# Two PSUM banks taken as one tile for a linear-attention head pair, and the split work and loads reordered around it

## The chip, the cores and the metric

The kernel runs on one core of a Trainium2 chip. The metric is the device time of one execution, in microseconds. Engines are called PE (TensorE, matrix products), DVE (VectorE), ACT (ScalarE), POOL (GpSimd) and SP (SyncE, which here only issues DMAs). PSUM is the memory that PE's products go to; a one-bank tile here has 512 fp32 values per partition.

## The reference, cut to what matters

```python
# q, k, v: (8 batches, 8 heads, 576 positions, 64)
kv = np.einsum('bhsd,bhse->bhde', k, v)
out = np.einsum('bhsd,bhde->bhse', q, kv)
rms = np.sqrt(np.mean(out * out, axis=-1, keepdims=True) + 1e-06)
x = (out / rms * g_norm)            # then (B,H,S,D) -> (B*S, H*D) = 4608 x 512
h = x @ w_in                        # w_in 512 x 2048
sp = np.maximum(h, 0.0) + np.log1p(np.exp(-np.abs(h)))
g = h * erf(sp)
return g @ w_out                    # w_out 2048 x 512
```

Attention without softmax: per head a 64x64 product of k and v, q times it, a normalisation over the 64 channels. Then a two-layer network with the activation h * erf(softplus(h)).

## The kernel before, in words

**Tokens.** They are worked in nine groups T of 512 columns. T=0 to 7 are the first 512 positions of each batch; T=8 holds the remaining 64 positions of all eight batches, whose attention outputs are collected in `x_last`. Everything is kept transposed: channels on partitions, tokens along the free axis.

**Precision.** T=0 runs its network in plain fp32. From T=1 on, f>=2 (`WHOLE`), each fp32 operand is written as fp32r forms (an upper part, a lower part, a combination), and `product` (L443 to 463) makes a 128x512 block as 12 fp32r matmuls: eight into `n_ps`, four into `m_ps`. DVE adds the two (`add` L439, `add_scaled` L434). The forms of an operand are made by ACT (upper, L399) and DVE (lower and combination, L402, L405). The weights' forms are made in the T=1 stage, by `w_upper` on ACT (L423) and `w_lower` on DVE (L426, L429), and written to DRAM; from then on `load_parts` (L589) fetches them block by block on SP's queue.

**Stages.** The main loop (L638 to 735) takes n = 0 to 31: T=0 for n<16, T=1 for n=16 to 31, with f = n mod 16 the block of 128 hidden channels. Then come the periods m = 8 to 36, four per group for T=2 to 8 (L780 to 853). A period has four hidden blocks (x times w_in; the softplus and erf on ACT; h times the result on DVE, L848) and four result blocks of the period before it (h times w_out).

**Attention.** While group T is worked, the attention of T+1 is made, one pair of heads p at a time (four pairs per group): a pair per period, and in the T=1 stage a pair at f = 0, 4, 8 and 12. Its pieces are those that `attention` (L265 to 394) returns:
- `products`: k times v into `kv_ps` (L293), for even pairs also a transpose of the q of the last 64 positions (L301); DVE copies the two 64x64 blocks into the block-diagonal `bd_kv` (L308) and, in even pairs, the transposed tail q (L311); PE transposes the q of 512 positions into `qt_ps` (L315) and ACT copies it out (L316).
- `apply`: `bd_kv` times the tail (L320, 64 columns) and times qT (L321, 512 columns, into `se_ps`), in fp32; DVE copies the tail's result to `x_last` (L322), ACT squares the rest (L324).
- `halve`: DVE splits the squares into two fp32r parts (L334, L335). `mean`: PE averages over channels (L342, L343, into `ms_ps`); ACT takes logarithm, exponential and square (L354 to 356). `norm`: three DVE instructions end in x (L362, L365, L374). `split`: the forms of x (L399, L402, L405).

`kv_ps`, `qt_ps`, `se_ps` and `ms_ps` are one-bank tiles that take turns in a pool of two. The remaining six banks serve the blocks.

**Order.** Nothing is reordered by a scheduler: each engine runs its instructions in the order in which the code calls them (`manual_schedule`). Semaphore waits are added where one engine touches a tile that another has written or read. In a period the pieces stand at places:

```python
places = (0, 2, 3, 5, 6, 8)      # products, apply, halve, mean, norm, split; place i+1 is behind block i
FETCH = ("", "in", "in", "out", "in", "out", "in", "out out")
```

So products come ahead of the first hidden block, apply behind the second, halve behind the third, mean behind the first result block. The split of a period's x comes behind its last result block, that is, in the queues of ACT and DVE just ahead of what the next products ask of them. The k, v and q of two pairs on are issued on SP's queue by `products_and_loads` (L387), at place 0.

In the T=1 stage each step f calls: the pieces due, the hidden block, ACT's copy of h and softplus (L702), the gating of an earlier block, `w_lower` of the blocks begun and `w_upper` of the blocks in `to_cut[f]`, then pieces again. `places_w` (L616) names the steps in which w_out blocks are split that stay in a place of their own in SBUF.

Of the kernel before, what the change touches and what calls it, by code (L numbers as in the profile page):

```python
# [39 lines left out]
FP32 = mybir.dt.float32  # L40
# [3 lines left out]
AF = mybir.ActivationFunctionType  # L44
ALU = mybir.AluOpType
PSUM = bass.MemoryType.PSUM
# [14 lines left out]
def kernel(  # L61
# [31 lines left out]
    first_w = room.enter_context(tc.tile_pool(name="first_w", bufs=1, side="right"))  # L93
    gate = room.enter_context(tc.tile_pool(name="gate", bufs=7, side="right"))
    early = early_room.enter_context(tc.tile_pool(name="early", bufs=2))
    ps_at = ctx.enter_context(tc.tile_pool(name="ps_at", bufs=2, space=PSUM))
    ps_h = ctx.enter_context(tc.tile_pool(name="ps_h", bufs=2, space=PSUM))
    ps_o = ctx.enter_context(tc.tile_pool(name="ps_o", bufs=1, space=PSUM))

    ctx.enter_context(tc.manual_schedule())  # L100

# [160 lines left out]

    xT, x_forms, tails = {}, {}, {}

    def attention(T, p, pools=None):  # L265

        st = {}

        halves = FIRST <= T < B
        bd = bd_kv[:, (T * NP + p) % 2, :]  # L270

        q_tail, o_tail = slice(P, 2 * P), slice(2 * P, 2 * P + R)

        def bank(name):
            pool, tag = (pools or {}).get(name, (ps_at, "at"))
            return pool.tile([P, G], FP32, name=name, tag=tag)

        def square_tile(name):

            if T == 0:  # L280
                return gate.tile([P, G], FP32, name=name, tag="h")
            return attp.tile([P, G], FP32, name=name, tag="qT")

        def products():

            kv_ps = st["kv"] = bank("kv_ps")
            ks, vs, qs = (x.pop((T, p)) for x in (k_sb, v_sb, q_sb))
            C = chunks(T)
            for c in range(C):
                rows = slice(0, S // C + (c < S % C))  # L290
                for i in range(2):
                    s = slice(i * D, i * D + D)
                    nc.tensor.matmul(  # L293
                        kv_ps[s, s],
                        lhsT=ks[rows, i, c],
                        rhs=vs[rows, i, c],
                        start=(c == 0),
                        stop=(c == C - 1),
                    )
            if p % 2 == 0:  # L300
                nc.tensor.transpose(kv_ps[:, q_tail], q_last[:, p // 2], ident)  # L301
            if p == NP - 2:
                for i in range(NP):
                    load_last(T + 1, i)
            st["qT"] = square_tile("qT")
            for i in range(2):
                s = slice(i * D, i * D + D)
                nc.vector.tensor_copy(out=bd[s, s], in_=kv_ps[s, s])  # L308
            if p % 2 == 0:
                tails[T] = attp.tile([P, P], FP32, name="qT_last", tag="t")  # L310
                nc.vector.tensor_copy(out=tails[T], in_=kv_ps[:, q_tail])  # L311
            st["tail"] = tails[T][:, p % 2 * R : p % 2 * R + R]
            qt_ps = bank("qt_ps")
            for j in range(J):
                nc.tensor.transpose(qt_ps[:, j * P : j * P + P], qs[:, j], ident)  # L315
            nc.scalar.copy(st["qT"], qt_ps)  # L316

        def apply():
            qT, o_ps, kv_ps = st["qT"], bank("se_ps"), st.pop("kv")
            nc.tensor.matmul(kv_ps[:, o_tail], lhsT=bd, rhs=st.pop("tail"), start=True, stop=True)  # L320
            nc.tensor.matmul(o_ps, lhsT=bd, rhs=qT, start=True, stop=True)  # L321
            nc.vector.tensor_copy(out=x_last[:, p, T * R : T * R + R], in_=kv_ps[:, o_tail])  # L322
            st["o"] = o_ps
            nc.scalar.activation(qT, o_ps, AF.Square)  # L324

        def square():
            st["o"], st["qT"] = x_last[:, p, :], square_tile("sq")
            nc.scalar.activation(st["qT"], st["o"], AF.Square)

        def halve():  # L330
            sq = st.pop("qT")
            hi = st["hi"] = attp.tile([P, G], FP32R, name="sq_hi", tag="rms_r")
            lo = st["lo"] = attp.tile([P, G], FP32R, name="sq_lo", tag="sq_lo")
            nc.vector.tensor_copy(out=hi, in_=sq)  # L334
            nc.vector.tensor_tensor(out=lo, in0=sq, in1=hi.bitcast(FP32), op=ALU.subtract)  # L335

        def mean(table=True):
            ms = st["ms"] = bank("ms_ps")
            if halves:


                nc.tensor.matmul(ms, lhsT=mean_w, rhs=st.pop("hi"), start=True, stop=False)  # L342
                nc.tensor.matmul(ms, lhsT=mean_w, rhs=st.pop("lo"), start=False, stop=True)  # L343
                u = square_tile("u")
            else:
                u = st.pop("qT")
                nc.tensor.matmul(ms, lhsT=mean_w.bitcast(FP32), rhs=u, start=True, stop=True)
            if T > 0:
                r = attp.tile([P, G], FP32, name="rms_r", tag="rms_r")
                exp_ln_table()  # L350
            else:
                r = gate.tile([P, G], FP32, name="rms_r", tag="s")
            st["u"], st["r"] = u, r
            nc.scalar.activation(r, ms, AF.Ln, bias=eps_col)  # L354
            nc.scalar.activation(r, r, AF.Exp, scale=-0.5)
            nc.scalar.activation(u, r, AF.Square)
            if table and (T > 0 or p == NP - 1):
                softplus_table()

        def norm():  # L360
            ms, u, r = (st.pop(name) for name in ("ms", "u", "r"))
            nc.vector.scalar_tensor_tensor(  # L362
                out=u, in0=ms, scalar=EPS, in1=u, op0=ALU.add, op1=ALU.mult
            )
            nc.vector.scalar_tensor_tensor(  # L365
                out=u, in0=u, scalar=3.0, in1=r, op0=ALU.subtract, op1=ALU.mult
            )
            if T < FIRST:
                if T not in xT:
                    xT[T] = wide.tile([P, KC, G], FP32, name="xT", tag="h")  # L370
                x = xT[T][:, p, :]
            else:
                x = st["x"] = x_new.tile([P, G], FP32, name="x", tag="x")
            nc.vector.scalar_tensor_tensor(  # L374
                out=x,
                in0=st.pop("o"),
                scalar=gm_col,
                in1=u,
                op0=ALU.mult,
                op1=ALU.mult,  # L380
            )

        def split():
            if T >= FIRST:
                thirds(st.pop("x"), *(form[:, p] for form in x_forms[T]))

        def products_and_loads():  # L387
            products()
            load_pair(T * NP + p + 2)

        if T == 0:
            return products, apply, halve, mean, norm
        first = (products_and_loads, apply) if T < B else (lambda: None, square)
        return (*first, halve if halves else lambda: None, mean, norm, split)


    def upper(x, high):
# [215 lines left out]

    others = [("in", f) for f in range(WHOLE)]
    others += [("out", f) for f in (*range(FC - BATCH, FC), *range(FC - BATCH))]
    places_w = {4: 0, 5: 1, 8: 0, 9: 1, FC - 4: 0, FC - 3: 1}  # L616
    to_cut = {f: [] for f in range(FC)}
    for f in range(FC):
        if f < FC - BATCH:
            to_cut[f] = [("in", f + WHOLE), others.pop(0)]  # L620
        elif f == FC - BATCH:
            to_cut[f] = [("in", FC - 2), ("in", FC - 1)]
        if f in places_w:
            to_cut[f].append((*others.pop(0), places_w[f]))
# [13 lines left out]
    for n in range(FIRST * FC + 1):  # L638
        T, f = divmod(n, FC)
        if n == FC:  # L640
            early_room.close()
            late = ctx.enter_context(tc.tile_pool(name="late", bufs=1))
            x_new = ctx.enter_context(tc.tile_pool(name="x_new", bufs=1))
            acc = ctx.enter_context(tc.tile_pool(name="acc", bufs=1))
            w_in_p = ctx.enter_context(tc.tile_pool(name="w_in_p", bufs=BATCH))
            low = low_room.enter_context(tc.tile_pool(name="low", bufs=1))
            forms = late.tile([P, 3, KC, G], FP32R, name="x_forms0")
            x_forms[FIRST] = [forms[:, i] for i in range(3)]
# [43 lines left out]
        if T < FIRST:  # L692
# [6 lines left out]
            else:  # L699
                nc.scalar.activation(h, n_ps, AF.Copy, scale=SHIFT - 1.0)  # L700
                add(h, m_ps)
            nc.scalar.activation(s, h, AF.Softplus)  # L702
            if T == FIRST - 1:
                if f == 1:
                    x_both = wide.tile([P, KC, G], FP32R, name="x_both", tag="h")
# [5 lines left out]
                    w_lower(*key)  # L711
                for key in to_cut[f]:
                    w_upper(*key)
            if n == 0:
                w_next("split")
            for piece in steps[f][1]:
# [63 lines left out]
    for m in range(first_batch, batches + 1):  # L780
# [9 lines left out]
        def piece():  # L790
            if todo:
                todo.pop(0)()
# [95 lines left out]
```

## Time and profile before

| | |
|---|---|
| median of 11 runs | 959.39 us (957.81 to 960.97) |
| profiled execution | 961.9 us, span 960.1 us |
| mean granted PE clock | 0.996 |
| busy: PE, DVE, ACT | 932.9, 740.8, 616.1 us |
| DMA | 259.78 MB, mean 271 GB/s |
| start of a period's k-v product to the next | 24.84 and 24.72 us in turn (m=10 on) |
| attention of the T=1 stage starts at | 146.69, 175.23, 206.06, 236.38 us |
| m=8 and m=9 start at | 261.89 and 286.74 us |

Times in the profile are microseconds from the start of the span. A timeline row is: start, duration, engine, line, operation, output tile <- input tiles, shapes, count, and in brackets how long the engine stood idle before it and what ended that. A row of waits is: engine, tile and line that waited, what it waited for, total us, times, longest. PEld is PE's loading of weights, SPq the issue of a DMA on SP's queue.

### The profile page before, as it was taken

What the parts mean: (1) busy time and instruction counts of PE and PEld (TensorE: products, weight loads), DVE (VectorE), ACT (ScalarE), POOL (GpSimd) and SP (SyncE); (2) the same over time, 40 slices, a digit from 0 to 9 for tenths busy, and PEclk for the clock granted to TensorE, in tenths of its full rate; (3) what the DMA queues carried; (4) which work ended last, traced back from release to release, by engine and by line L of the source; (5) the groups of instructions that cost most, each with busy time, mean ns of one, the idle gap of its engine ahead of it and who ended that gap; (6) DMA issues with size and microseconds to landing.
All of it is one profiled execution on the core that took longest, in us unless ns stands there. A gap on an engine that the chain in (4) does not pass through costs nothing.

```text
span 960.1 us, 11752 instructions
## 1 busy us (share of the span) xinstructions
PE 932.9 (97%) x4272; PEld 686.4 (71%) x4272; DVE 740.8 (77%) x1054; ACT 616.1 (64%) x825; POOL 2.4 (0%) x10
## 2 busy tenths in 40 slices
PE   6999999989998999999999999999999999999998
PEld 4344445556586888888888888888888788878886
DVE  2979958777675888888878887878787877778667
ACT  3889875677663666666666666666666666665552
POOL 0000000000000000000000000000000000000000
PEclk9999999999998999999999999999999999999999
DMA  9756505688899887889888978988897779768872
GB/s 253 262 159 216 174 10 233 228 317 303 293 306 329 312 310 276 249 306 339 296 261 322 325 289 279 322 316 289 271 341 266 262 244 352 274 258 298 338 273 67
DMA packets 111842, 259.78 MB, mean 271 GB/s; under 512 B 43864, under 2 KB 69544, under 8 KB 111784
## 3 DMA queue, kind: packets, MB, share of 16 engines
q1 hardware_dynamic: 110152, 256.73, 76.1%
q10 hardware_dynamic: 1568, 2.29, 0.8%
q8 instruction: 34, 0.56, 0.2%
q14 instruction: 24, 0.20, 0.1%
q0 software_dynamic: 64, 0.00, 0.0%
HBM read 224.40 MB, written 34.60 MB: 270 GB/s over the span
## 4 chain that ended last, share of the span: by engine, by line
PE 79%; DVE 8%; ACT 8%; DMA 3%; issue 1%; SPq 0%; DVEq 0%; ACTq 0%
PE n_ps L456 42%; PE m_ps L456 21%; PE o_ps L514 5%; PE h_ps L685 3%; PE se_ps L321 2%; PE kv_ps L293 2%; PE qt_ps L315 1%; DMA out_dram<-e 1%; DMA w_out<-w_new 1%; ACT s_sb L720 1%; DMA v_sb<-in_v_dram 1%; ACT L103 1%; DVE h L848 1%; ACT w_e L215 1%; DMA q_last<-in_q_dram 1%
## 5 line engine op out<-in xcount | busy, mean ns | idle before, releaser
L456 PE MATMUL n_ps<-x_forms,w_in_parts 128*128 128x512 f32 x896 | 235.0, 404 | 5.5 <-ACT h L828 4.0
L456 PE MATMUL n_ps<-w_out_parts,g_forms 128*128 128x512 f32 x928 | 231.5, 391 | 0.0
L456 PEld LDWEIGHTS n_ps<-x_forms,w_in_parts 128*128 128x128 f32 x896 | 167.7, 189 | 50.0 <-issue 8.8
L456 PEld LDWEIGHTS n_ps<-w_out_parts,g_forms 128*128 128x128 f32 x928 | 174.5, 188 | 38.6 <-issue 1.4
L830 ACT ACTIVATE s<-h 128x512 f32<-128x512 f32 x112 | 71.1, 635 | 178.9 <-DVE h L439 178.9
L439 DVE TENSOR_TENSOR h<-m_ps,h 128x512 f32<-128x512 f32 x116 | 79.8, 688 | 65.5 <-ACT h L828 41.4
L456 PE MATMUL m_ps<-w_out_parts,g_forms 128*128 128x512 f32 x464 | 124.2, 389 | 0.0
L456 PE MATMUL m_ps<-x_forms,w_in_parts 128*128 128x512 f32 x448 | 120.8, 392 | 0.0
L514 PE MATMUL o_ps<-w_out_sb,h_sb 128*128 128x512 f32 x224 | 100.8, 593 | 0.3 <-DVE h_sb L636 0.3
L456 PEld LDWEIGHTS m_ps<-w_out_parts,g_forms 128*128 128x128 f32 x464 | 87.1, 188 | 18.1
L456 PEld LDWEIGHTS m_ps<-x_forms,w_in_parts 128*128 128x128 f32 x448 | 84.7, 189 | 17.9
L439 DVE TENSOR_TENSOR e<-m_ps,e 128x512 f32<-128x512 f32 x116 | 80.2, 692 | 17.8 <-PE m_ps L456 10.9
L434 DVE SCALAR_TENSOR_TENSOR e<-n_ps,e 128x512 f32<-128x512 f32 x88 | 60.3, 685 | 38.8 <-PE n_ps L456 38.7
L514 PEld LDWEIGHTS o_ps<-w_out_sb,h_sb 128*128 128x128 f32 x224 | 42.3, 190 | 48.9 <-issue 46.6
L828 ACT ACTIVATE h<-n_ps 128x512 f32<-128x512 f32 x112 | 65.5, 585 | 14.0 <-DMA q_sb<-in_q_dram 10.1
L405 DVE SCALAR_TENSOR_TENSOR g_forms<-g_forms 128x1024 fp32r<-128x1024 f32 x58 | 71.1, 1226 | 2.0
L402 DVE TENSOR_TENSOR g_forms<-h,g_forms 128x1024 fp32r<-128x1024 f32 x58 | 70.6, 1218 | 1.7 <-ACT g_forms L399 1.4
L399 ACT ACTIVATE g_forms<-h 128x1024 fp32r<-128x1024 f32 x58 | 58.9, 1060 | 12.4 <-PE m_ps L456 9.8
L848 DVE TENSOR_TENSOR h<-h,s 128x1024 f32<-128x1024 f32 x56 | 65.9, 1218 | 0.7 <-ACT s L834 0.7
L685 PE MATMUL h_ps<-xT,w_in_sb 128*128 128x512 f32 x144 | 64.9, 594 | 0.8 <-DVE w_in_sb L240 0.6
L106 ACT ACT_TABLE_LOAD x44 | 56.5, 1283 | 0.7
L834 ACT ACTIVATE s<-s 128x1024 f32<-128x1024 f32 x56 | 56.3, 1052 | 0.3
(98 smaller groups left out, 1017.3 us busy)
## 6 DMA issues: line engine op xcount, KB each, us to landing
w_out_parts<-w_out SPq DMA_DIRECT2D x116, 768.0 KB
w_in_parts<-w_in SPq DMA_DIRECT2D x112, 768.0 KB
w_in<-w_new SPq DMA_DIRECT2D x16, 768.0 KB
q_sb<-in_q_dram SPq DMA_DIRECT2D x32, 256.0 KB
w_raw<-in_moe_w_out_dram SPq DMA_DIRECT2D x8, 1024.0 KB
out_dram<-e SPq DMA_DIRECT2D x32, 256.0 KB
k_sb<-in_k_dram SPq DMA_DIRECT2D x28, 287.5 KB
v_sb<-in_v_dram SPq DMA_DIRECT2D x28, 287.5 KB
```

The source lines that it names most:

```text
L106: nc.scalar.preload_act_table_set("softplus")
L399: nc.scalar.activation(high, x, AF.Copy, scale=1.0 + 2.0**-13)
L402: nc.vector.tensor_tensor(out=low, in0=x, in1=high.bitcast(FP32), op=ALU.subtract)
L405: nc.vector.scalar_tensor_tensor(out=both, in0=low.bitcast(FP32), scalar=SHIFT, in1=high.bitcast(FP32), op0=ALU.mult, op1=ALU.add,)
L434: nc.vector.scalar_tensor_tensor(out=out_, in0=ps, scalar=scale, in1=out_, op0=ALU.mult, op1=ALU.add)
L439: nc.vector.tensor_tensor(out=out_, in0=ps, in1=out_, op=ALU.add)
L456: nc.tensor.matmul(ps, lhsT=weights(form, k), rhs=moving(form, k), start=(form == forms[0] and k == 0), stop=(form == forms[-1] and k == 3),)
L514: nc.tensor.matmul(o_ps[j], lhsT=g[:, j * P : j * P + P], rhs=w_out_sb[:, f, :], start=(f == 0), stop=last,)
L685: nc.tensor.matmul(plain[i], lhsT=w_in_sb[:, c, i % FC * P : i % FC * P + P], rhs=xT[T][:, c, :], start=(c == 0), stop=(c == KC - 1),)
L828: nc.scalar.activation(h[:, i], n_ps, AF.Copy, scale=SHIFT - 1.0)
L830: nc.scalar.activation(s[:, i], h[:, i], AF.Softplus)
L848: nc.vector.tensor_tensor(out=part(h, half), in0=part(h, half), in1=part(s, half), op=ALU.mult)
```

## The change

There are five edits.

1. From T=2 on, a pair has one PSUM tile `at_ps` of two banks (`two_banks`, pool `ps_two`, one buffer) in place of four one-bank tiles. kv and the transposed tail q are in bank 0, the transposed q in bank 1; later the product fills the first 288 columns of both banks, and the mean the last 256.
2. For T=2 to 7 the tail's 64 columns ride with the 512: qT is a tile of 2 x 288 columns (256 and half of the tail), and the block-diagonal product is two matmuls of 288 columns. DVE copies the tail's columns into qT; in even pairs it also keeps the 64 columns of the next pair (`qT_next`). The mean is four fp32r matmuls of 256 columns in place of two of 512. Elementwise work runs over a 2 x 256 view.
3. The loads of k, v and q move from `products` to `halve`: in a period from place 0 to place 3, behind the first two w_in parts; in the T=1 stage from f = 0, 4, 8, 12 to f = 2, 6, 10, 14.
4. `to_cut` takes a step's other block ahead of its w_in block, and `places_w` has other steps and a third place.
5. In the T=1 stage the softplus (L702) is called behind the `w_upper` calls of its step.

```diff
@@ -93,9 +93,11 @@
-    ps_at = ctx.enter_context(tc.tile_pool(name="ps_at", bufs=2, space=PSUM))
     ps_h = ctx.enter_context(tc.tile_pool(name="ps_h", bufs=2, space=PSUM))
     ps_o = ctx.enter_context(tc.tile_pool(name="ps_o", bufs=1, space=PSUM))
+
+    at_room = ctx.enter_context(ExitStack())
+    ps_at = at_room.enter_context(tc.tile_pool(name="ps_at", bufs=2, space=PSUM))
...
+    def chain(*pieces):
+        for piece in pieces:
+            piece()
+
...
         def bank(name):
+            if T >= FIRST:
+                return two_banks()[:, name in ("qt_ps", "se_ps")]
             pool, tag = (pools or {}).get(name, (ps_at, "at"))
             return pool.tile([P, G], FP32, name=name, tag=tag)
-        def square_tile(name):
+        def two_banks():
+            if "two" not in st:
+                st["two"] = ps_two.tile([P, 2, G], FP32, name="at_ps", tag="at")
+            return st["two"]
+
+
+
+        HG, HR = G // 2, R // 2
+
+        def twofold(x):
+            return x.rearrange("p (i n) -> p i n", i=2) if halves else x
+
+        def square_tile(name, tail=False):
             if T == 0:
                 return gate.tile([P, G], FP32, name=name, tag="h")
-            return attp.tile([P, G], FP32, name=name, tag="qT")
+            t = attp.tile([P, 2, HG + HR], FP32, name=name, tag="qT")
+            if tail:
+                return t
+            return t[:, :, :HG] if halves else t.rearrange("p i n -> p (i n)")[:, :G]
...
-            st["qT"] = square_tile("qT")
+            st["qT"] = square_tile("qT", halves)
             for i in range(2):
                 s = slice(i * D, i * D + D)
                 nc.vector.tensor_copy(out=bd[s, s], in_=kv_ps[s, s])
-            if p % 2 == 0:
-                tails[T] = attp.tile([P, P], FP32, name="qT_last", tag="t")
-                nc.vector.tensor_copy(out=tails[T], in_=kv_ps[:, q_tail])
-            st["tail"] = tails[T][:, p % 2 * R : p % 2 * R + R]
+            if halves:
+                tail = tails.pop(T) if p % 2 else kv_ps[:, P : P + R]
+                nc.vector.tensor_copy(out=st["qT"][:, :, HG:], in_=twofold(tail))
+                if p % 2 == 0:
+                    tails[T] = attp.tile([P, R], FP32, name="qT_next", tag="t")
+                    nc.vector.tensor_copy(out=tails[T], in_=kv_ps[:, P + R : 2 * P])
+            else:
+                if p % 2 == 0:
+                    tails[T] = early.tile([P, P], FP32, name="qT_last", tag="t", bufs=1)
+                    nc.vector.tensor_copy(out=tails[T], in_=kv_ps[:, q_tail])
+                st["tail"] = tails[T][:, p % 2 * R : p % 2 * R + R]
             qt_ps = bank("qt_ps")
             for j in range(J):
                 nc.tensor.transpose(qt_ps[:, j * P : j * P + P], qs[:, j], ident)
-            nc.scalar.copy(st["qT"], qt_ps)
+            if halves:
+                nc.scalar.copy(st["qT"][:, :, :HG], twofold(qt_ps))
+            else:
+                nc.scalar.copy(st["qT"], qt_ps)
         def apply():
+            if halves:
+                qT, two = st.pop("qT"), two_banks()
+                del st["kv"]
+                for i in range(2):
+                    nc.tensor.matmul(
+                        two[:, i, : HG + HR], lhsT=bd, rhs=qT[:, i], start=True, stop=True
+                    )
+                nc.vector.tensor_copy(
+                    out=twofold(x_last[:, p, T * R : T * R + R]), in_=two[:, :, HG : HG + HR]
+                )
+                o_ps = st["o"] = two[:, :, :HG]
+                qT = st["qT"] = qT[:, :, :HG]
+                nc.scalar.activation(qT, o_ps, AF.Square)
+                return
             qT, o_ps, kv_ps = st["qT"], bank("se_ps"), st.pop("kv")
             nc.tensor.matmul(kv_ps[:, o_tail], lhsT=bd, rhs=st.pop("tail"), start=True, stop=True)
             nc.tensor.matmul(o_ps, lhsT=bd, rhs=qT, start=True, stop=True)
...
-            nc.vector.tensor_copy(out=hi, in_=sq)
-            nc.vector.tensor_tensor(out=lo, in0=sq, in1=hi.bitcast(FP32), op=ALU.subtract)
+            nc.vector.tensor_copy(out=twofold(hi), in_=sq)
+            nc.vector.tensor_tensor(
+                out=twofold(lo), in0=sq, in1=twofold(hi.bitcast(FP32)), op=ALU.subtract
+            )
         def mean(table=True):
-            ms = st["ms"] = bank("ms_ps")
+            ms = st["ms"] = two_banks()[:, :, HG:] if halves else bank("ms_ps")
             if halves:
-                nc.tensor.matmul(ms, lhsT=mean_w, rhs=st.pop("hi"), start=True, stop=False)
-                nc.tensor.matmul(ms, lhsT=mean_w, rhs=st.pop("lo"), start=False, stop=True)
+                hi, lo = (twofold(st.pop(name)) for name in ("hi", "lo"))
+                for i in range(2):
+                    nc.tensor.matmul(ms[:, i], lhsT=mean_w, rhs=hi[:, i], start=True, stop=False)
+                    nc.tensor.matmul(ms[:, i], lhsT=mean_w, rhs=lo[:, i], start=False, stop=True)
                 u = square_tile("u")
...
             if T > 0:
-                r = attp.tile([P, G], FP32, name="rms_r", tag="rms_r")
+                r = twofold(attp.tile([P, G], FP32, name="rms_r", tag="rms_r"))
                 exp_ln_table()
...
-                out=x,
+                out=twofold(x),
...
-        def products_and_loads():
-            products()
+        def loads():
             load_pair(T * NP + p + 2)
         if T == 0:
             return products, apply, halve, mean, norm
-        first = (products_and_loads, apply) if T < B else (lambda: None, square)
-        return (*first, halve if halves else lambda: None, mean, norm, split)
+        if T == B:
+            return lambda: None, square, lambda: None, mean, norm, split
+
+        pieces = ((products,), (apply,), (halve, loads)) if halves else ((products, loads), (apply,), ())
+        return (*(partial(chain, *group) for group in pieces), mean, norm, split)
...
     others = [("in", f) for f in range(WHOLE)]
     others += [("out", f) for f in (*range(FC - BATCH, FC), *range(FC - BATCH))]
-    places_w = {4: 0, 5: 1, 8: 0, 9: 1, FC - 4: 0, FC - 3: 1}
+    places_w = {3: 0, 5: 1, 6: 0, 8: 1, 9: 2, 10: 0}
     to_cut = {f: [] for f in range(FC)}
     for f in range(FC):
         if f < FC - BATCH:
-            to_cut[f] = [("in", f + WHOLE), others.pop(0)]
+            to_cut[f] = [others.pop(0), ("in", f + WHOLE)]
         elif f == FC - BATCH:
             to_cut[f] = [("in", FC - 2), ("in", FC - 1)]
         if f in places_w:
@@ -639,6 +692,8 @@
...
         if n == FC:
             early_room.close()
+            at_room.close()
+            ps_two = ctx.enter_context(tc.tile_pool(name="ps_two", bufs=1, space=PSUM))
             late = ctx.enter_context(tc.tile_pool(name="late", bufs=1))
...
-            nc.scalar.activation(s, h, AF.Softplus)
             if T == FIRST - 1:
...
@@ -711,6 +765,7 @@
                     w_lower(*key)
                 for key in to_cut[f]:
                     w_upper(*key)
+            nc.scalar.activation(s, h, AF.Softplus)
```

## The prediction

> **What bounds the kernel now.** I read the busy shares first, then the chain that ended last, then the waits of the tensor engine (PE), then the timeline of one period, then the windows around the one odd stretch.
>
> The page's busy times, and the chain's shares by engine:
>
> ```profile
> PE 932.9 (97%) x4272; PEld 686.4 (71%) x4272; DVE 740.8 (77%) x1054; ACT 616.1 (64%) x825; POOL 2.4 (0%) x10
> PE 79%; DVE 8%; ACT 8%; DMA 3%; issue 1%; SPq 0%; DVEq 0%; ACTq 0%
> ```
>
> PE sets the time: 97% busy and four fifths of the chain. A microsecond in which PE stands still is added to the end. The vector engine (DVE) has 23% to spare on average, which says nothing about where it stands when PE comes to need it. The waits of PE (total us, times, longest):
>
> ```profile
> PE n_ps L456 <- ACT h L828: 4.0, 1, 4.0
> ...
> PEld kv_ps L293 <- DVE x L374: 6.0, 17, 0.4
> ```
>
> The second is the only regular one: 17 times at most 0.4 us, where a period's first product (k with v) waits until the pair before has left its PSUM bank. So in each period DVE's normalised x ends just as PE arrives. The timeline of one period end (start, duration; the first three lines are the period before):
>
> ```profile
> 517.55 0.60 PE L315 MATMUL qt_ps<-ident,q_sb 128*128 128x128 f32 x4
> 520.43 0.45 DVE L308 COPY bd_kv<-kv_ps 64x64 f32<-64x64 f32 x2
> 520.89 0.29 DVE L311 COPY qT_last<-kv_ps 128x128 f32<-128x128 f32 x1
> ...
> 536.16 0.69 DVE L439 TENSOR_TENSOR e<-m_ps,e 128x512 f32<-128x512 f32 x1 [0.22 <-PE m_ps L456]
> 536.77 2.35 DVE L848 TENSOR_TENSOR h<-h,s 128x1024 f32<-128x1024 f32 x2
> 539.04 0.68 DVE L362 SCALAR_TENSOR_TENSOR u<-ms_ps,u 128x512 f32<-128x512 f32 x1
> 539.76 0.69 DVE L365 SCALAR_TENSOR_TENSOR u<-u,rms_r 128x512 f32<-128x512 f32 x1
> 540.49 0.75 DVE L374 SCALAR_TENSOR_TENSOR x<-se_ps,gm_col,u 128x512 f32<-128x512 f32 x1
> 541.15 0.68 DVE L434 SCALAR_TENSOR_TENSOR e<-n_ps,e 128x512 f32<-128x512 f32 x1
> 541.50 0.80 PE L293 MATMUL kv_ps<-v_sb,k_sb 116*64 116x64 f32 x20
> 541.94 0.69 DVE L439 TENSOR_TENSOR e<-m_ps,e 128x512 f32<-128x512 f32 x1
> 542.23 0.66 PE L315 MATMUL qt_ps<-ident,q_sb 128*128 128x128 f32 x4
> 542.55 0.68 DVE L434 SCALAR_TENSOR_TENSOR e<-n_ps,e 128x512 f32<-128x512 f32 x1
> 543.33 0.69 DVE L439 TENSOR_TENSOR e<-m_ps,e 128x512 f32<-128x512 f32 x1
> 543.94 0.68 DVE L402 TENSOR_TENSOR x_forms<-x,x_forms 128x512 fp32r<-128x512 f32 x1
> 544.66 0.69 DVE L405 SCALAR_TENSOR_TENSOR x_forms<-x_forms 128x512 fp32r<-128x512 f32 x1
> 545.27 0.45 DVE L308 COPY bd_kv<-kv_ps 64x64 f32<-64x64 f32 x2
> ```
>
> PE runs kv (541.50), the q transposes (542.23) and goes on. DVE copies kv out (L308) only at 545.27, because four additions and two x_forms stand ahead of it in its queue. Today that hurts nobody: the product that needs the copy comes two hidden blocks later. The one long stall and what follows it (window, its length, busy us and count of PE, PEld, DVE, ACT, POOL, granted clock, DMA share, GB/s):
>
> ```profile
> 295.00:301.00 6.00, 2.43 (x11) 1.67 (x9) 0.00 (x0) 0.21 (x1) 0.00 (x0) 0.94 0.68 241
> 301.00:307.10 6.10, 5.66 (x13) 4.46 (x14) 4.11 (x6) 3.10 (x6) 0.00 (x0) 0.50 0.97 253
> ```
>
> PE stands for 4.2 us (behind ScalarE's h, itself behind a store that landed late) and then runs at half clock to 307.1.
>
> **What the Trainium skill says.** "PSUM — Partial Sum Buffer", section "PSUM bank collisions raise a hardware error": accesses of two engines must be kept apart by bank and quadrant, and ScalarE and VectorE queues are strict FIFO (next section, "Engine vs sequencer instructions"). The trace agrees with the FIFO part (L308 leaves at 545.27 although its input was there at 542.3). By the bank rule PE could write bank 1 of the new two-bank tile while DVE reads bank 0. But the built order of the changed kernel has the wait: the q transposes into `at_ps` wait for DVE's last copy out of `at_ps`, the second bd copy in odd pairs and the qT_next copy in even ones. In the kernel before they wait for DVE's x of the last pair alone, since kv and q have tiles of their own. "TensorE: Matmul & The Clock Gate", Part 1: the clock halves after at least one idle window of about 3.4 us, and windows run freely. The stall above agrees: 4.2 us idle, then 0.50.
>
> **The change part by part.** A period of the changed kernel is a closed loop, because PE now waits for DVE, which waits for PE:
> - PE from the transposes to the end of the second result block: 517.55 to 536.13 (what L439 waits for), 18.6 us. The new products take four passes of 288 columns for two of 512 (0.430 each start to start in this trace) and two of 64 (0.110): by columns 4 x 0.242 = 0.97 against 1.08. Four mean passes of 256 (0.12 by columns) stand for two of 512 (0.2275): 0.48 against 0.455. Net -0.08: 18.53.
> - DVE from there to the end of x: 536.16 to 541.24, 5.08 us, all back to back.
> - DVE from x to the end of the bd copies: 541.24 to 545.72, 4.48 us, again back to back.
> - Odd pairs: one semaphore hop, an estimate of 0.06 (x ends at 541.24 and ScalarE starts on it at 541.27; PE has weights to load besides). Even pairs: two small copies first. By start-to-start 0.13 plus a length of 0.215 (the 64-column copy L322 has mean 216 ns): 0.35.
>
> Sum: 28.15 us (odd) and 28.50 (even), against 24.68 (542.23 - 517.55) and 24.88 before. Added: 3.47 and 3.62. PE stands about 3.7 us before each set of transposes, and all matmuls queued behind wait with it: eight blocks of the period, so the ScalarE and DVE work on them. Periods m=9 to 27 are 10 odd and 9 even: 34.7 + 32.6 = 67.3 us.
>
> The five other sets of products, by the same reading (bd copies' end against PE's transposes): f=0 1.1 us, f=4 3.0, f=8 4.2, f=12 1.6, m=8 2.2; sum 12.1. Gaps of PE right there (1.10 at 179.3, 0.81 at 207.3, 1.15 at 211.2, each waiting for ScalarE's q copy or near it) run inside the new waits: -3.1. Together +9.0.
>
> Softplus behind the weights' upper forms, the new order of splits and w_out's places: the same instructions in the T=1 stage (630 and 616 ns each). ScalarE waits there 18.5 us for h; the moves fill those waits. What PE could win is its other gaps (1.4 and 0.5): between -2 and, if a softplus two to three upper forms later holds up the gating, +3; I take -1.
>
> Moving k, v, q loads behind two w_in parts: the same DMAs on SP's queue, some 8 us (three blocks) later. They are for two pairs on, 49 us before use, so the cover is still about 40 us. If it were gone, 0.83 MB at some 300 GB/s is 2.8 us a period. w_in parts move ahead; PE has no regular wait on them. Zero, bounds -1 and +3. The stall at 297: PE comes later by then while the store goes on landing, so most of 4.2 us and of some 3 us lost to half clock go: -6 (0 to -7).
>
> Half clock behind the new waits: the trace has one example, 5.7 us at half speed after the stall, 2.9 us lost. A stand of 3.7 us holds a free-running window of 3.4 us whole in about one case of ten: 20 x 0.12 x 2.9 = 7; bounds 0 and 58 (every time).
>
> Sum: 67.3 + 9.0 - 1 - 6 + 7 = +76. The profiled execution has 961.9 us (span 960.1), the median of the 11 runs is 959.4; the difference is carried to the median: 1036.
>
> **Rivals.**
> - *Half clock after nearly every wait.* For: the one long stall did it, and a threshold below "wholly idle" would make 3.7 us with a few small matmuls enough. Against: gaps of 1.1 to 1.4 us didn't. 1036 - 7 + 58 = 1087.
> - *DVE gains on PE while PE stands.* If x ended 1.5 us or more ahead of kv, the additions of the third block would be done too, and bd would end 2.8 us after kv (two pieces of addition, two x_forms, the copy): about 2.1 us a period, 40 in all, and 1008. Against: L848 and with it x hang on the second result block, and everything after is back to back.
> - *Faster: the waits are met in time and the smaller products count.* 24 x 0.08 = 2, T=1 stage 2 to 4, the stall at 297 up to 7: 948 to 955, 950 as its value. It decides if DVE's copy ends within 0.1 us of PE's arrival at the transposes; it is 3.5 us behind in every period of the trace.
> - *The change does nothing:* the same, with the gains near zero: 959.
>
> **How the numbers follow.** The stated loop 0.66 (own range 1020 to 1055), half clock each time 0.16, DVE gaining 0.13, faster 0.03, nothing 0.02 (of which half is slower). Two in ten outside leaves 1003 to 1085: it takes in the third case and the lower half of the second. 0.2% (about 2 us) is about what a measurement of this kernel tells from no change. Faster 0.03, same 0.01, slower 0.96.
>
> **What would show it.** Right: PE's waits list the transposes (L345) behind DVE's bd copy and the qT_next copy, 24 times, 3 to 4 us each; PE's share falls to about 90%; periods are 28.1 and 28.5 us; m=28 on is unchanged; the stall near 297 is gone or small. The granted clock tells the second case from the first (0.99 against some 0.93). Wrong: a period under 27, or PE's transposes starting before DVE's bd copies end.

## The result and the profile after

The changed kernel takes 1063.95 us (median of 8 runs, 1060.41 to 1066.6) against 959.39 us: the ratio is 1.1083, 95% interval 1.107 to 1.1095. It is 10.8% slower. The profiled execution has 1061.0 us, its span is 1059.3 us; the span of the kernel before was 960.1 us, so 99.2 us are to be explained.

Busy times and the chain's shares by engine, after:

```profile
PE 966.7 (91%) x4320; PEld 719.1 (68%) x4320; DVE 745.7 (70%) x1078; ACT 623.7 (59%) x825; POOL 2.4 (0%) x10
PE 55%; DVE 19%; issue 1%; ACT 1%; DVEq 0%
```

PE's busy share falls from 97% to 91%, and DVE's share of the chain rises from 8% to 19% (the shares of the chain after add up to 76% of the span, so this understates it): the path to the end now runs through DVE. PE is also busy 34 us longer, although the change takes work from it. Both show in the next two views. The waits of PE (total us, times, longest):

```profile
PE at_ps L345 <- DVE bd_kv L331: 38.0, 12, 3.5
PE at_ps L345 <- DVE qT_next L337: 36.2, 12, 3.6
```

These are the q transposes. They wait 24 times, once for each of the 24 pairs with products: odd pairs for the bd copy, even pairs for the qT_next copy. Before, neither row existed. One period of the changed kernel, DVE and PE (start, duration):

```profile
616.25 0.69 DVE L492 TENSOR_TENSOR e<-m_ps,e 128x512 f32<-128x512 f32 x1 [0.21 <-PE m_ps L509]
616.86 2.35 DVE L903 TENSOR_TENSOR h<-h,s 128x1024 f32<-128x1024 f32 x2
...
620.57 0.75 DVE L425 SCALAR_TENSOR_TENSOR x<-at_ps,gm_col,u 128x512 f32<-128x512 f32 x1
...
625.35 0.45 DVE L331 COPY bd_kv<-at_ps 64x64 f32<-64x64 f32 x2
625.81 0.22 DVE L334 COPY qT<-at_ps 128x64 f32<-128x64 f32 x1
625.95 0.21 DVE L337 COPY qT_next<-at_ps 128x64 f32<-128x64 f32 x1
...
621.58 0.80 PE L316 MATMUL at_ps<-v_sb,k_sb 116*64 116x64 f32 x20
622.31 0.33 PE L324 MATMUL at_ps<-ident,q_last 128*128 128x128 f32 x1
626.22 1.11 PE L345 MATMUL at_ps<-ident,q_sb 128*128 128x128 f32 x4 [3.58 <-DVE qT_next L337]
```

DVE works without a gap from the addition behind the second result block (616.25) to the qT_next copy (626.16), 9.9 us, and PE's transposes start 0.06 us later. That is the chain that the prediction summed: 5.08 + 4.48 + 0.35 = 9.9. What the sum gave too small a place is in the windows of the same period (window, length, busy us and count of PE, PEld, DVE, ACT, POOL, granted clock, DMA share, GB/s):

```profile
621.58:622.60 1.02, 1.02 (x22) 0.80 (x21) 0.92 (x2) 0.41 (x1) 0.00 (x0) 1.00 0.87 241
622.60:624.36 1.76, 0.04 (x1) 0.00 (x0) 1.73 (x4) 0.00 (x0) 0.00 (x0) 1.00 0.89 363
624.36:626.22 1.86, 0.00 (x1) 0.01 (x1) 1.67 (x6) 0.00 (x0) 0.00 (x0) 0.50 0.35 135
626.22:631.20 4.98, 4.98 (x14) 4.11 (x15) 2.22 (x2) 2.91 (x4) 0.00 (x0) 0.50 0.02 7
631.20:636.00 4.80, 4.80 (x22) 3.89 (x22) 4.06 (x6) 1.65 (x4) 0.00 (x0) 1.00 0.62 179
```

Some 1.8 us into this wait the granted clock halves, and it stays at 0.50 for 6.83 us. For the 4.98 us behind the wait PE does 14 matmuls; at full clock it does 22 in 4.80. The mean clock is 0.951, before it was 0.996.

The starts of the transposes split the 99.2 us. Where no block is slow, a period lasts 28.22 us (ending with an odd pair) or 28.59 (even), against 24.67 and 24.88. For the 19 periods from m=8's transposes to those of m=27 that is 10 x 3.55 + 9 x 3.71 = 68.9 us. The same 19 periods have 574.1 us in the trace, 34.6 more than at those lengths (10 x 28.22 + 9 x 28.59 = 539.5): this is the half clock: 144 block matmuls start up to 0.43 us apart for 0.227 (27 us), and the transposes in front of them are slow too. The long stall of the kernel before at 297 is gone, with its own slow blocks: the period in which it stood had 31.85 us for 24.88, so 7.0. From the k-v product of f=0 to the transposes of f=12 the T=1 stage takes 91.45 us for 90.42, 1.0 more; m=8 adds 2.1, and half clock behind the last pair adds 1.6. Ahead of f=0, where both kernels do the same work, this execution of the kernel before is 2.0 us slower than this one of the changed kernel (146.69 for 144.69; 144.2 to 145.4 in the traces of all experiments), which has nothing to do with the change. 68.9 + 34.6 - 7.0 + 1.0 + 2.1 + 1.6 - 2.0 = 99.2. The medians are 104.6 us apart: the profiled execution of the changed kernel lies 2.9 us under its median, that of the kernel before 2.5 us over.

### The profile page after: what moved, and what is told of

Same layout as the page of the kernel before. It is cut to its first block, busy times and chain, and to the rows that moved or that the text cites. A ratio compares the mean times of both kernels' runs of the same rounds, so it can differ in the third digit from the quotient of the medians.

```text
span 1059.3 us, 11956 instructions
## 1 busy us (share of the span) xinstructions
PE 966.7 (91%) x4320; PEld 719.1 (68%) x4320; DVE 745.7 (70%) x1078; ACT 623.7 (59%) x825; POOL 2.4 (0%) x10
## 4 chain that ended last, share of the span: by engine, by line
PE 55%; DVE 19%; issue 1%; ACT 1%; DVEq 0%
PE n_ps L509 34%; PE m_ps L509 16%; DVE h L903 4%; DVE e L492 4%; PE at_ps L356 2%; PE at_ps L345 2%; DVE e L487 2%; DVE x L425 1%; DVE u L416 1%; DVE x_forms L458 1%; DVE x_forms L455 1%; DVE u L413 1%; DVE bd_kv L331 1%; DVE e L824 1%; PE at_ps L394 0%
## 5 line engine op out<-in xcount | busy, mean ns | idle before, releaser
L509 PE MATMUL n_ps<-x_forms,w_in_parts 128*128 128x512 f32 x896 | 256.1, 432 | 1.6 <-DVE x_forms L455 0.8
L509 PEld LDWEIGHTS n_ps<-x_forms,w_in_parts 128*128 128x128 f32 x896 | 183.7, 208 | 43.6 <-DVE x_forms L455 1.6
L509 PE MATMUL m_ps<-x_forms,w_in_parts 128*128 128x512 f32 x448 | 126.7, 407 | 0.0
L509 PEld LDWEIGHTS m_ps<-x_forms,w_in_parts 128*128 128x128 f32 x448 | 91.1, 203 | 21.2
L345 PE MATMUL at_ps<-ident,q_sb 128*128 128x128 f32 x96 | 21.9, 368 | 74.2 <-DVE bd_kv L331 38.0
L347 ACT COPY qT<-at_ps 128x512 f32<-128x512 f32 x24 | 14.1, 586 | 106.4 <-PE at_ps L345 106.4
L345 PEld LDWEIGHTS at_ps<-ident,q_sb 128*128 128x128 f32 x96 | 13.9, 182 | 78.1 <-DVE bd_kv L331 39.7
```

The costliest lines, as they stand in the source:

```text
L509: nc.tensor.matmul(ps, lhsT=weights(form, k), rhs=moving(form, k), start=(form == forms[0] and k == 0), stop=(form == forms[-1] and k == 3),)
```

## The experiments

**Theory.** PE waits for DVE only because, in the order of the calls, DVE's copies out of `at_ps` stand ahead of the transposes into it; the wait makes a loop PE - DVE - PE of 28.15 and 28.5 us; the half clock is a second term which the wait brings. **Rivals:** the single two-bank tile holds the loop by another path; the wide products and their extra copies do it; the blocks are slow for a reason of their own. Experiments 2, 3, 4 and 8 ran once each; what is read from them is 28 us and more, and the runs of the changed kernel lie within 6.2 us.

**1. Order of the calls undone.** The tile, the products and all other edits stay.

```diff
             st["qT"] = square_tile("qT", halves)
+            qt_ps = bank("qt_ps")
+            for j in range(J):
+                nc.tensor.transpose(qt_ps[:, j * P : j * P + P], qs[:, j], ident)
+            if halves:
+                nc.scalar.copy(st["qT"][:, :, :HG], twofold(qt_ps))
+            else:
+                nc.scalar.copy(st["qT"], qt_ps)
             for i in range(2):
                 s = slice(i * D, i * D + D)
                 nc.vector.tensor_copy(out=bd[s, s], in_=kv_ps[s, s])
...
-            qt_ps = bank("qt_ps")
-            for j in range(J):
-                nc.tensor.transpose(qt_ps[:, j * P : j * P + P], qs[:, j], ident)
...
```

> The changed kernel with PE's q transposes and ScalarE's copy of them called ahead of DVE's copies out of the same tile; nothing else. My theory (PE waits for DVE only because of this order, and the slow clock comes from that wait): PE's waits at the transposes go from 78 us in 24 to under 2, periods come back to 24.6 and 24.8 us, no half clock from m=10 on, and the time is 945 to 957 us, at or a little under the kernel before. Rival (the two-bank tile with one buffer holds the loop by another path, ScalarE's copy or the square): periods above 25.5 and above 980 us.

Measured: 952.72 us, ratio to the kernel before 0.9924 (0.9902 to 0.9945). Periods are 24.61 and 24.82 us, clock 1.00; PE's longest waits from m=8 on are two of one stretch, at 293 and 311:

```profile
PE n_ps L509 <- ACT h L883: 2.1, 1, 2.1
PE at_ps L316 <- issue: 1.6, 1, 1.6
```

The wait at L345 is no longer in the list, and all 111 us between the two versions come from an order of calls. Under this order the tile costs nothing in a period, and the wide products save 0.06 us a period.

**2. PE freed, ScalarE left behind DVE.** As 1, but the ScalarE copy of q stays where the changed kernel has it.

```diff
             st["qT"] = square_tile("qT", halves)
+            qt_ps = bank("qt_ps")
+            for j in range(J):
+                nc.tensor.transpose(qt_ps[:, j * P : j * P + P], qs[:, j], ident)
             for i in range(2):
...
-            qt_ps = bank("qt_ps")
-            for j in range(J):
-                nc.tensor.transpose(qt_ps[:, j * P : j * P + P], qs[:, j], ident)
             if halves:
                 nc.scalar.copy(st["qT"][:, :, :HG], twofold(qt_ps))
```

> As the first run, but ScalarE's copy of the transposed q is left behind DVE's copies, so that PE is free and ScalarE waits for DVE instead. Theory: PE doesn't stand at the transposes, but ScalarE's g_forms come some 2.5 us later and DVE's behind them; about 1.2 to 1.6 us a period are lost, 26.0 us each, no half clock, 980 to 992 us. Rival (ScalarE has slack enough, PE's own wait was all of it): the time of the first run within 3 us.

Measured: 981.1 us, periods 26.23 and 26.32, clock 0.998. ScalarE's waits and PE's:

```profile
ACT qT L347 <- DVE qT_next L340: 43.6, 12, 4.3
ACT qT L347 <- DVE bd_kv L334: 41.0, 11, 3.9
...
PE at_ps L316 <- issue: 27.0, 18, 1.6
```

The wait has moved to ScalarE. It reads bank 1 and DVE reads bank 0, and neither writes the tile: the waits that the build adds go by the tile and not by the bank, here as for PE in the changed kernel. PE loses only 1.6 us a period, now in front of the k-v product (L316). "issue" there is a wait whose releaser the profile does not name; the timeline tells it: in the period at 545, DVE waits 1.69 us for ScalarE's u, its x ends at 545.72, and the product, which needs the tile that x reads, starts at 545.82. So ScalarE's lateness reaches PE through x. No half clock follows these stands.

**3. PE kept busy while it waits.** 20 matmuls, used by nobody, into a free part of bank 0 behind the k-v product (pairs of T=3 to 7).

```diff
                 nc.tensor.transpose(kv_ps[:, q_tail], q_last[:, p // 2], ident)
+            if halves and T > FIRST:
+                for i in range(20):
+                    nc.tensor.matmul(
+                        kv_ps[:, 2 * P :], lhsT=mean_w, rhs=x_forms[T - 1][0][:, i % KC, : 2 * P], start=True, stop=True
+                    )
```

> The changed kernel with 20 fp32r matmuls of 256 columns (0.12 us each, 2.4 us) put behind the k-v product of the periods, into a part of the first bank that is free then; their results are used by nobody. PE waits for DVE as before, but is busy for most of that time. Theory: the waits and the slow clock are two terms. Periods are 28.2 and 28.6 us throughout, as those of the changed kernel without slow blocks are, the granted clock is 0.99 or more, and the time 1020 to 1030 us. Rival (the blocks are slow for another reason, such as weights that arrive late, or the filler delays the wait's end): periods of 30.5 us or more and 1060 to 1110 us.

Measured: 1027.43 us, clock 0.996, periods 28.20 to 28.23 and 28.55 to 28.60 from m=10 on. The wait's end and the windows up to it and behind it:

```profile
660.42 2.63 PE L327 MATMUL at_ps<-x_forms,mean_w 128*128 128x256 f32 x20
664.25 0.66 PE L350 MATMUL at_ps<-ident,q_sb 128*128 128x128 f32 x4 [1.20 <-DVE qT_next L342]
```

```profile
660.40:664.25 3.85, 2.65 (x23) 2.45 (x22) 3.63 (x9) 0.00 (x0) 0.00 (x0) 1.00 0.76 283
664.25:671.00 6.75, 6.75 (x32) 5.59 (x33) 4.41 (x5) 4.10 (x6) 0.00 (x0) 1.00 0.34 106
```

The transposes start when they did, as DVE lets them, and the clock stays at 1.00. Useless work on PE makes this kernel 36.5 us faster. So the wait and the half clock are two terms, and the second is the size that was read from the trace.

**4. The tile alone.** The kernel before, with one two-bank tile from T=2 on and nothing else.

```diff
...
         def bank(name):
+            if T >= FIRST:
+                if "two" not in st:
+                    st["two"] = ps_two.tile([P, 2, G], FP32, name="at_ps", tag="at")
+                return st["two"][:, name in ("qt_ps", "se_ps")]
...
```

> The kernel before with one edit: from T=2 on the four one-bank tiles are one tile of two banks. Products of 64 and 512 columns, loads and the order of the T=1 stage are as before. Theory: this edit alone makes the loss; PE waits 3.2 to 3.6 us at the transposes of nearly every pair (22 to 24 times), half clock follows most, and the time is 1040 to 1070 us. Rival (the 288-column products and the copies for them make the loop long): 955 to 975 us.

Measured: 1065.6 us, clock 0.954.

```profile
PE at_ps L320 <- DVE bd_kv L313: 40.3, 12, 3.5
PE at_ps L320 <- DVE qT_last L316: 37.1, 12, 3.5
```

The same 24 waits, and within 2 us the same time: this edit makes the loss, under the old order of calls.

**5 to 7. The other edits, one at a time.** Loads alone: in the kernel before, the call `load_pair(T * NP + p + 2)` moved from behind `products` to behind `halve` for T=2 to 7. T=1 edits alone: `to_cut`, `places_w` and the softplus as in the change. Wide products alone: experiment 1 with loads, splits and softplus put back.

```diff
...
+        if halves:
+            return products, apply, halve_and_loads, mean, norm, split
         first = (products_and_loads, apply) if T < B else (lambda: None, square)
...
```

> The kernel before with one edit: the loads of k, v and q called behind the halving of the squares (for T=2 to 7). Theory (they are hidden with some 40 us to spare): no change in the steady periods, 24.67 and 24.89 us; at most the stretch of 290 to 312 us shifts, where DMA is full: 956 to 961 us against 960. Rival (they get in the way of the w_out parts fetched behind them): PE waits on w_out_parts, above 963 us.

> The kernel before with the edits of the T=1 stage alone: softplus behind the weights' upper forms, the order of the splits, w_out's places. The first run's T=1 stage (first q transposes to those of m=8) was 110.4 us against 115.2; if these edits made that, it is 110 to 111.5 here too and the time is 953 to 957 us. Rival (the reordered product made it, by freeing ScalarE's wait on q): 114 to 115.5 and 958 to 961 us.

> The two-bank tile and the 288-column products, with PE's transposes and ScalarE's copy ahead of DVE's copies as in the first run, but loads, softplus and splits where the kernel before has them. Theory: 0.07 us a period less PE work, 24.60 and 24.82 us, some 2 us in all, 956 to 959 us. Rival (two banks with one buffer cost something in the T=1 stage): above 960 us.

Measured against 959.79: 955.85 us for the loads (ratio 0.9952, 0.9939 to 0.9964), 960.48 for the T=1 edits (1.0003, 0.9992 to 1.0013), 961.71 for the wide products (1.0019, 1.0013 to 1.0026). All three expected ranges were missed. The loads came out 0.15 us under theirs, and only 0.9 us of their gain is in the stretch named there (30.94 us for 31.85): the rest is earlier. From the transposes of f=0 to those of m=8 the kernel takes 111.45 us for 115.20. In that stage (146 to 262 us) the kernel before has these waits on ScalarE, and the loads' kernel has neither:

```profile
ACT w_new L423 <- DMA w_in<-w_new: 2.4, 1, 2.4
...
ACT w_new L423 <- DMA w_out<-w_new: 1.2, 1, 1.2
```

`w_upper` waits for a weight tile whose store is in SP's queue. In the kernel before, q, k and v stand there between the output stores of T=0 and the next store of a weight tile, which is issued 6.1 us behind the first of them (178.01 to 184.08); with the loads two steps later it is 2.9 us (176.58 to 179.49). The T=1 edits alone gain nothing: their stage takes 118.1 us, and the same wait is longer there:

```profile
ACT w_new L423 <- DMA w_out<-w_new: 7.1, 2, 5.2
```

The wide products alone save 0.07 us a period as worked out, but lose more in the T=1 stage (118.3 us for 115.2), where PE comes to wait for DVE's copies and halves:

```profile
PE at_ps L356 <- DVE qT L341: 2.4, 2, 1.8
PE at_ps L356 <- DVE qT_next L344: 2.2, 1, 2.2
PE at_ps L393 <- DVE sq_hi L381: 1.7, 2, 0.9
```

**8. The wait made shorter.** In the changed kernel, for 15 pairs, the split of x is put off behind the next pair's DVE copies.

```diff
...
+        def late_split():
+            if FIRST < T < B and p < NP - 1:
+                put_off.append(split)
+            else:
+                split()
...
-        pieces = ((products,), (apply,), (halve, loads)) if halves else ((products, loads), (apply,), ())
-        return (*(partial(chain, *group) for group in pieces), mean, norm, split)
+        pieces = ((products, put_off_split), (apply,), (halve, loads)) if halves else ((products, loads), (apply,), ())
+        return (*(partial(chain, *group) for group in pieces), mean, norm, late_split)
```

> The changed kernel, PE's wait on DVE kept, but shorter: in 15 of the 20 periods with products the split of x (ScalarE's upper form, DVE's two forms) is called behind DVE's copies for the next pair and no longer ahead of them. The loop as I sum it loses DVE's two forms, 1.3 us: 26.9 and 27.2 us where no block is slow, and PE stands about 2.3 us at the transposes of these pairs. If the half clock goes by the length of the stand, it is gone there, and the time is 1064 - 20 - about 30 = 1010 to 1020 us. If any stand of 2 us brings it, periods are 29 to 29.7 us and the time 1040 to 1048. Rival to the loop (the period is set by ScalarE and DVE in another way): periods within 0.5 us of the changed kernel's 28.2 to 31.

Measured: 1019.84 us, clock 0.980. Periods without slow blocks are 26.88 to 26.89 and 27.23 to 27.24: the loop shrank by the 1.3 us of the two instructions, as summed. Before the transposes of these pairs PE starts nothing for 2.4 to 2.7 us (2.1 to 2.4 from the end of its last matmul); half clock (a granted clock of 0.50) follows in 7 of the 15, and in all 4 of the other pairs from m=12 on, where PE stands 3.9 us. In the changed kernel, with 3.7 to 3.9 us, it follows in 17 of 19, and in experiment 3, with 1.2 to 1.5 us, never. So at the shorter stand it was neither gone nor there every time, and length alone doesn't tell the cases apart.

Where the stand falls in time does. The 19 half-clock stretches of the changed kernel's trace begin at 177.22, 293.28, 320.58 us and so on, and all of these starts lie on one grid of 3.413 us, to within 0.001. Three stands of that kernel, cut along the grid (columns as above):

```profile
470.77:474.18 3.41, 1.65 (x25) 1.08 (x23) 3.20 (x6) 0.63 (x1) 0.00 (x0) 1.00 0.76 281
474.18:477.60 3.42, 1.71 (x10) 1.48 (x11) 1.80 (x5) 1.02 (x2) 0.00 (x0) 1.00 0.28 114
501.49:504.90 3.41, 0.42 (x5) 0.42 (x5) 2.77 (x8) 0.00 (x0) 0.00 (x0) 1.00 0.45 185
504.90:508.32 3.42, 3.42 (x11) 2.74 (x9) 1.43 (x2) 2.49 (x3) 0.00 (x0) 0.50 0.00 0
620.96:624.37 3.41, 1.68 (x25) 1.03 (x23) 3.27 (x6) 0.63 (x1) 0.00 (x0) 1.00 0.90 333
624.37:627.78 3.41, 1.56 (x6) 1.47 (x7) 1.66 (x6) 0.41 (x1) 0.00 (x0) 0.50 0.21 81
627.78:631.20 3.42, 3.42 (x9) 2.65 (x9) 2.22 (x2) 2.50 (x4) 0.00 (x0) 0.50 0.00 2
```

The grid splits the first stand into 1.76 and 1.71 us without a matmul, and the clock stays. The second has 2.99 us in one window: half clock in the next, which is busy throughout, then full clock again. The third has 1.73 and 1.85 us: half clock, and a second window of it, since PE was idle in the first as well. Taken over all 13 traces of this case from 100 us on, half clock began behind 43 of 43 windows with 1.94 us or more of idle time, 23 of 35 with 1.66 to 1.93, and 1 of 131 with 0.5 to 1.63 (idle time by the trace's matmul ends, which are modelled). Once there it went on behind all 27 windows with 0.66 us of idle time or more, and ended behind all 56 with 0.56 or less. In experiment 8 the seven stands that brought it have 1.72 to 2.24 us in one window, in the eight others the largest part in one window is 1.29 to 1.74. What decides between 1.66 and 1.93 us is open.

**9 to 11. What goes together, and the best version.** 9: experiment 7 with the loads moved. 10: the kernel before with loads and T=1 edits, no wide tile. 11: experiment 1, with T=1's output stores issued by GpSimd.

```diff
-            nc.sync.dma_start(out=rows[:, j, :], in_=e)
+            (nc.gpsimd if T == FIRST - 1 else nc.sync).dma_start(out=rows[:, j, :], in_=e)
```

> The reordered kernel of the first run (two-bank tile, 288-column products, transposes ahead of DVE's copies) without the edits of softplus, splits and w_out's places; the loads of k, v and q behind the halving. If each edit adds up, it is the wide-only kernel less the 3.9 us of the loads: 957 to 958.5. If the edits of the T=1 stage are needed with the wide tile (their gain is seen only together), it is 4 us or more above the first run's 952.7.

> The kernel before with the loads moved and the edits of the T=1 stage, without the two-bank tile. If the wide tile and the wide products gain nothing, 952 to 954, as the first run; if the T=1 edits gain nothing without the wide tile, 955.5 to 957, as the loads alone.

> The first run's kernel, with the four output stores of group T=1 issued by GpSimd instead of SP, so that they don't stand in one queue with the weight loads. In the first run ScalarE's h waits 8.1 us for the last of these stores, which was issued at 283.0 and landed at about 292.4, and PE stands 2.2 us, then 0.9, 0.5 and 1.8 us, with some 4 us of slow blocks. If the queue makes the store late, PE's stands at 290 to 310 go and the time is 945 to 950. If the stores are late because all DMA is busy there, no change: 951 to 955.

Measured against 959.71: 959.94 us (1.0005, 0.9997 to 1.0014), 953.39 (0.9933, 0.992 to 0.9946) and 950.01 (0.9901, 0.9885 to 0.9917). The effects do not add: the T=1 edits are worth nothing alone, some 2.5 us with the loads moved, some 7 on top of the wide tile and the loads. Within the intervals, the whole gain of experiment 1 over the kernel before can be had without the two-bank tile (10). In 11 ScalarE's wait for the stores is shorter, and PE's stand of 2.1 us behind it is gone. The wait in experiment 1, then in 11:

```profile
ACT h L883 <- DMA out_dram<-e: 8.1, 1, 8.1
ACT h L883 <- DMA out_dram<-e: 6.1, 1, 6.1
```

The period in which it stands takes 28.40 us for 30.40. Three shorter gaps of PE (0.7, 0.3 and 1.6 us between 296 and 308) stay, and 950.01 lies at the edge of the range for a late queue. The slow blocks that the expectation counts in experiment 1 are not in its trace: from 276 to 312 the clock is 1.00. 11 has the lowest median, 1% under the kernel before; its interval and that of experiment 1 (0.9902 to 0.9945) overlap, so the lead of 11 over 1 rests on the trace more than on the times.

## Why the prediction was right, and where it was off

**Direction, place and mechanism: right.** PE waits at the transposes for exactly the two copies named, 24 times. Experiments 1 and 4 show it from both sides: the tile alone makes the loss, the order of calls alone takes it away.

**The loop: right.** 28.15 and 28.50 us were forecast; 28.22 and 28.59 were measured; the 19 periods' sum was 67.3 and is 68.9. Experiment 8 moved it by the forecast 1.3 us.

**Half clock: the term that was mis-sized.** The step that failed is "A stand of 3.7 us holds a free-running window of 3.4 us whole in about one case of ten", which gave 7 us. Measured: 34.6 us in the 19 periods and 1.6 behind them; experiment 3 takes 36.5 us off by itself. A window need not be idle whole: in the changed kernel 1.66 to 2.99 us of idle time in a window of 3.41 brought the half clock, behind 17 of 19 stands and not one in ten. The cost of one event was put too high: 2.9 us forecast, 1.5 to 2.5 in the trace. The Trainium skill ("TensorE: Matmul & The Clock Gate", Part 1) has the clock drop after at least one idle window of about 3.4 us, and the window run freely. The traces agree with the free-running window and its length (the grid of 3.413 us); they differ if "idle" means wholly idle. The one example that the prediction drew on could have told it: the stall of the kernel before is 4.0 us long, but the window of 3.41 us that ends where the clock halves, at 300.32, has PE idle for 2.9 us of it:

```profile
296.91:300.32 3.41, 0.52 (x3) 0.10 (x1) 0.00 (x0) 0.00 (x0) 0.00 (x0) 1.00 0.55 175
```

The rival "half clock after nearly every wait" had the frequency, and it named the reason, a threshold below "wholly idle". At 1087 it counted 2.9 us each and no gain in the T=1 stage. The granted clock, which was to tell the two cases apart (0.99 against some 0.93), is 0.951, nearer to the rival's. The measured 1064 lies above the stated loop's own range, 1020 to 1055, and inside the wide one, 1003 to 1085, because that was drawn to take in part of this rival. The loop was understood; that the total held is in part luck.

**Stall at 297: right.** -6 forecast, -7.0 measured; it is gone.

**T=1 stage and m=8: half right.** m=8 was forecast at +2.2 and is +2.1. For f=0 to 12, +5.8 was forecast (9.9 of waits, -3.1 of gaps, -1 for the edits) and +1.0 was measured. The waits there are 5.1 us, not 9.9; why DVE comes sooner to its copies in that stage was not followed. The other edits were worth more than was counted: with the wait out (experiment 1) the same stretch takes 85.69 us, 4.7 less than before. The loads were costed at "zero, bounds -1 and +3", when alone they are worth 3.9 us: the step asked only whether k, v and q come in time, and not who stands behind them in SP's queue.

**Rivals.** "DVE gains on PE while PE stands" (1008) fails: x ends at 621.32, 0.26 us ahead of the k-v product, and periods without slow blocks are at the forecast loop. "Faster" and "nothing" fail as written; but the 948 to 955 of the former is what experiment 1 gives once the wait is out.

The sum between the traces: +76 forecast (67.3 + 2.2 + 5.8 - 6 + 7), +99 measured (68.9 + 2.1 + 1.0 - 7.0 + 36.2, and -2.0 ahead of f=0). 29 us of the difference is the half clock; nearly 5 fewer in the T=1 stage and the 2.0 go against it.

## What to carry to other kernels

When tiles are merged, look at every pair of accesses that were to different tiles and now are to one, and ask in which order the code calls them: a wait arises from the order, and swapping two calls can take it away at no cost. Price a wait on an engine that is late by following that engine's queue back to where it last stood idle. And where PE comes to stand in each period, don't ask whether a stand fills a window of 3.41 us whole, but how much of it falls into one window: a stand of 3.5 us puts 1.75 us or more into one of the two windows that it touches, and here that was enough in 17 of 19 cases. That is an estimate from this kernel's traces.

## What was unexpected of the hardware

- The granted clock halved after stands of 2.4 to 2.7 us in 7 of 15 cases, of 3.7 to 3.9 us in 17 of 19, of 1.2 to 1.6 us in none of the periods from m=10 to 27 of experiments 2 and 3 (one stretch of experiment 2 behind the last pair followed a window with gaps of 0.7 and 0.8 us, at 783 and 784). Where it did, blocks ran at 0.43 us a matmul for 0.227.
- The start and the end of half clock are judged differently: about half a window of idle time (1.66 us and more of 3.41) brought it, but it went on until a window had 0.56 us of idle time or less. So a stretch lasts 3.41 us where the stand is over when it begins, and 6.83 us where a good part of the stand still lies ahead, as at 624.37.
- In the changed kernel the half clock recurs in step with the work: from 562.93 to 747.25 it begins every 30.72 us, which is nine windows of 3.413, and periods of 30.5 and 31.0 us alternate. That the two lock to each other is argued from these numbers and was not tried.
- Filling such a stand with 2.4 us of useless matmuls made the kernel 3.4% faster (1063.95 to 1027.43).
